# The first layer of a dense mixture by seven block products in place of eight

## The chip, the cores and the metric

One Trainium2 chip, one of its cores. The metric is the time of one execution on the device in microseconds (us); of several runs the median is given.

## What is computed

Three stages in a row: causal attention over 2 batches of 8 heads (576 tokens, 64 channels), a top-1 mixture of 8 experts, and a dense mixture of 4 experts, each over 1152 tokens of 512 channels. The change is in the third stage and in what the second hands to it.

```python
def _moe2_ref(x, domain_probs, w1, w2):       # x [1152, 512], w1 [4, 512, 1024], w2 [4, 1024, 512]
    p = domain_probs / (domain_probs.sum(-1, keepdims=True) + 1e-09)
    out = np.zeros((N, D), dtype=np.float32)
    for e in range(E):
        h = np.maximum(x @ w1[e], 0.0)
        out += p[:, e:e + 1] * (h @ w2[e])
    return out.astype(np.float32)
```

## The kernel before

The kernel is written with a scheduling layer: the Python text gives the work and the tiles, the layer sets the order of the instructions on each engine, the places in memory and the semaphores. On the chip each engine then works through its own list in that order. A pool with `bufs=n` holds n tiles of a tag; an instruction that takes a tile waits until the tile's last holder has been read.

**Float32 by halves.** In the dense stage, and for one expert of the top-1 stage, a float32 operand is split into a rounded part (`hi`, `xh`, `hh`; type float32r, made by ScalarE, ACT) and the rest (`lo`, `xl`, `hl`; made by VectorE, DVE). A product is then three float32r matmuls: hi by hi, hi by low, low by hi. The other seven experts of the top-1 stage use float32 matmuls, which the trace shows as two records each.

**The top-1 stage** (lines 700 to 830). Tokens are sorted by expert; slot `sl` of 8 has a fixed capacity (`CAPS`). `layer1` (L733 on) multiplies 8 tiles of F into PSUM tiles `pg` (3 buffers), read by ACT and DVE in turn; `layer2` (L765 on) makes 4 tiles `py` (3 buffers), and `put_y` (L760) writes each into `xh` and `xl`, the transposed and sorted input of the dense stage: ACT first, then DVE. Expert weights come by DMA on SyncE's queue (SP), in tiles `w` of 128 x 1024 (512 KB) from the pool `wp`, 17 buffers. Behind the last slot stands a branch (`tc.If(most > 0)`, L832) for tokens over capacity, which is not taken here.

**The dense stage** (L861 to L891). For each of 4 experts `e`, and for each third `g` of the tokens (384): the first layer makes 8 tiles of F, each from 4 tiles of D by 3 products, 12 matmuls of 384 columns into `pg`; ACT takes `hh`, DVE takes `hl` from it. The second layer then makes 3 tiles of 128 tokens, 24 matmuls of 512 columns each into `py`; DVE scales by the token's probability and adds into `acc` (the tile `X`). The weights of the next expert are split while the present one is worked on (`load_w`, `split_w`, L683 to L689). After the last expert each tile of tokens is scattered to its place in the output by GpSimd (POOL).

```python
for f in range(FC):
    pg = ps.tile([P, 512], F32, tag="g1", name="pg", bufs=3)
    ...
    for cc in range(KC):
        for wt, xt in ((whi, xh), (whi, xl), (wlo, xh)):
            nc.tensor.matmul(out=pg[:, :GN], lhsT=wt[:, cc, fs], rhs=xt[:, cc, cs], start=n == 0, stop=n == 3 * KC - 1)
```

Of the kernel before, what the change touches and what calls it, by code (L numbers as in the profile page):

```python
# [9 lines left out]
F32 = mybir.dt.float32  # L10
# [22 lines left out]
G = 3  # L33
GN = N // G
# [347 lines left out]
def tile_attention_moe_moe(  # L382
# [5 lines left out]
    wp = ctx.enter_context(tc.tile_pool(name="wp", bufs=17))  # L388
# [3 lines left out]
    X = con.tile([P, NT, DM], F32, name="X")  # L392
# [196 lines left out]
    mp = ctx.enter_context(tc.tile_pool(name="mp", bufs=1))  # L589
    hp_ = ctx.enter_context(tc.tile_pool(name="hp", bufs=9))  # L590
    ps = ctx.enter_context(tc.tile_pool(name="ps", bufs=2, space=PSUM))
# [32 lines left out]
    xh = mp.tile([P, KC, XW], F32R, name="xh")  # L624
    xl = mp.tile([P, KC, XW], F32R, name="xl")
# [107 lines left out]
    def layer1(pa, xs, cap, load=None):  # L733
        xs, xsl = xs
        split = xsl is not None
        hb = mp.tile([P, FC, GN], F32R if split else F32, tag="hh", name="hb")
        hbl = mp.tile([P, FC, GN], F32R, tag="hl", name="hbl") if split else None
# [55 lines left out]
    def rest(j):  # L793

        if j != 1:
            return
        for i in range(4):
            t = wp.tile([P, 2, DM], F32, tag="w", name="w")
# [13 lines left out]
    xs = turn_first(xw)  # L812
    for sl in range(E1):
# [12 lines left out]
        if not last:  # L826
            pa, pb = na, nb_

    ha, hb2 = load_w(u1[0], u2[0], True)


    with tc.If(most > 0):  # L832
        with tc.For_i(0, E1, 1) as sl:
# [4 lines left out]
            with tc.For_i(0, ov_r, P) as i:  # L838
# [8 lines left out]
                for dc in range(KC):  # L847
# [5 lines left out]
                    put_y(dc, py[:, :P], oo, P)  # L853


    acc = X
    for e in range(E2):
        if e:
            ha, hb2 = load_w(u1[e], u2[e], True)
        for g in range(G):  # L860
            cs = slice(g * GN, (g + 1) * GN)  # L861
            hh = mp.tile([P, FC, GN], F32R, tag="hh", name="hh")
            hl = mp.tile([P, FC, GN], F32R, tag="hl", name="hl")
            for f in range(FC):
                pg = ps.tile([P, 512], F32, tag="g1", name="pg", bufs=3)
                fs = slice((f % 2) * P, (f % 2) * P + P)
                whi, wlo = ha[f // 2]
                n = 0
                for cc in range(KC):
                    for wt, xt in ((whi, xh), (whi, xl), (wlo, xh)):  # L870
                        nc.tensor.matmul(out=pg[:, :GN], lhsT=wt[:, cc, fs], rhs=xt[:, cc, cs], start=n == 0, stop=n == 3 * KC - 1)  # L871
                        n += 1
                nc.scalar.activation(out=hh[:, f, :], in_=pg[:, :GN], func=AF.Relu)  # L873
                nc.vector.scalar_tensor_tensor(out=hl[:, f, :], in0=pg[:, :GN], scalar=0.0, in1=hh[:, f, :].bitcast(F32), op0=ALU.max, op1=ALU.subtract)  # L874
            for t in range(GN // P):
                tt = g * (GN // P) + t
# [12 lines left out]
                if e == E2 - 1:
                    scatter("out", out, aux.bitcast(I32)[:, tt, 4:5], acc[:, tt, :])  # L890
# [27 lines left out]
```

## Time and profile before

| | |
|---|---|
| median of 3 runs | 731.23 us (730.08 to 731.41) |
| the profiled execution, own time | 736.14 us |
| its span in the profile | 734.5 us |
| TensorE (PE) busy | 709.0 us, 97% |
| VectorE (DVE) busy | 269.4 us, 37% |
| ScalarE (ACT) busy | 210.5 us, 29% |
| clock granted to TensorE, mean | 0.98 |

The span is cut into three stretches: attention and routing until about 160 us, the top-1 stage until 327 us, the dense stage until the end. Matmuls are pipelined: a record of 338 ns overlaps the next one, so that PE's rate is read from the distance of starts, not from the mean duration. Times inside the profile are of one execution, which was 4.9 us above the median.

### The profile page before, as it was taken

To read this page: it belongs to the slowest core of one execution; us is meant where nothing else is said; L and a number is where in the kernel's file an instruction comes from. 1 tells how busy PE (TensorE), PEld (TensorE's weight loads), DVE (VectorE), ACT (ScalarE), POOL (GpSimd) and SP (SyncE) were. 2 spreads that over 40 slices of the span, in tenths; PEclk is the share of its full clock that TensorE was granted. 3 is DMA by queue.
4 is the path that set the end of the run, shared out by engine and by line. 5 is a ranking of instruction groups with operands and counts; after the bars stand their busy time and mean duration, and the time that the engine had idled before them with its cause. 6 is when DMAs were issued, how large, how long until landed. Compare 5 with 4: busy or idle time off the path is not lost.

```text
span 734.5 us, 11018 instructions
## 1 busy us (share of the span) xinstructions
PE 709.0 (97%) x4349; PEld 648.2 (88%) x4350; DVE 269.4 (37%) x724; ACT 210.5 (29%) x435; POOL 33.3 (5%) x72
## 2 busy tenths in 40 slices
PE   8899999969899999999999999999999999999996
PEld 5799999859799999989899898989898998989895
DVE  7586767642127111432122341214231133412121
ACT  5577767511125111331011230104120121302010
POOL 2000000033200000000000000000000000010101
PEclk9999999979899999999999999999999999999999
DMA  6656764049978976440001230003210011000001
GB/s 145 178 129 173 190 162 136 1 174 330 359 233 296 326 254 202 148 169 2 1 0 30 87 114 1 1 1 114 87 29 0 1 47 40 0 29 15 29 15 44
DMA packets 87006, 78.83 MB, mean 107 GB/s; under 512 B 42699, under 2 KB 67275, under 8 KB 86951
## 3 DMA queue, kind: packets, MB, share of 16 engines
q1 hardware_dynamic: 83063, 72.76, 32.5%
q0 software_dynamic: 1776, 4.79, 1.7%
q10 hardware_dynamic: 2112, 0.52, 0.4%
q8 instruction: 36, 0.59, 0.3%
q14 instruction: 19, 0.16, 0.1%
HBM read 69.08 MB, written 8.99 MB: 106 GB/s over the span
## 4 chain that ended last, share of the span: by engine, by line
PE 53%; issue 1%; POOL 0%; POOLq 0%; DVE 0%
PE pg L871 27%; PE py L883 26%; POOL out_dram L402 0%; POOLq L913 0%; DVE X L888 0%; POOLq L402 0%
## 5 line engine op out<-in xcount | busy, mean ns | idle before, releaser
L871 PE MATMUL pg<-xh,hi 128*128 128x384 f32 x384 | 129.3, 337 | 1.8 <-PEq L832 1.8
L871 PE MATMUL pg<-xl,hi 128*128 128x384 f32 x384 | 129.6, 338 | 0.0
L871 PE MATMUL pg<-xh,wl 128*128 128x384 f32 x384 | 128.8, 335 | 0.0
L873 ACT ACTIVATE hh<-pg 128x384 fp32r<-128x384 f32 x96 | 47.2, 492 | 277.5 <-PE pg L871 277.5
L883 PE MATMUL py<-wl,hh 128*128 128x512 f32 x288 | 113.9, 395 | 0.0
L883 PE MATMUL py<-hi,hh 128*128 128x512 f32 x288 | 113.1, 393 | 0.0
L883 PE MATMUL py<-hi,hl 128*128 128x512 f32 x288 | 112.9, 392 | 0.0
L874 DVE SCALAR_TENSOR_TENSOR hl<-pg,hh 128x384 fp32r<-128x384 f32 x96 | 53.5, 558 | 122.0 <-ACT hh L873 120.2
L871 PEld LDWEIGHTS pg<-xh,hi 128*128 128x128 f32 x384 | 71.9, 187 | 2.5 <-ACTq L832 2.0
L871 PEld LDWEIGHTS pg<-xl,hi 128*128 128x128 f32 x384 | 72.3, 188 | 0.5
L871 PEld LDWEIGHTS pg<-xh,wl 128*128 128x128 f32 x384 | 72.1, 188 | 0.1
L750 PE MATMUL pg<-xs,w 128*128 128x128 f32 (+6 forms) x448 | 65.2, 308 | 3.1 <-issue 3.0
L750 PEld LDWEIGHTS pg<-xs,w 128*128 128x128 f32 x448 | 63.3, 202 | 4.4 <-issue 4.0
L883 PEld LDWEIGHTS py<-hi,hh 128*128 128x128 f32 x288 | 54.1, 188 | 12.5
L883 PEld LDWEIGHTS py<-hi,hl 128*128 128x128 f32 x288 | 54.0, 188 | 12.5
L883 PEld LDWEIGHTS py<-wl,hh 128*128 128x128 f32 x288 | 54.0, 188 | 11.6
L888 DVE SCALAR_TENSOR_TENSOR X<-py,aux,X 128x512 f32<-128x512 f32 x27 | 20.3, 751 | 117.5 <-PE py L883 117.5
L775 PE MATMUL py<-hb,w 128*128 128x128 f32 (+6 forms) x448 | 61.3, 295 | 0.0
L775 PEld LDWEIGHTS py<-hb,w 128*128 128x128 f32 x448 | 59.4, 190 | 0.2
L688 DVE TENSOR_TENSOR wl<-w,hi 128x1024 fp32r<-128x1024 f32 x40 | 48.9, 1224 | 24.3 <-ACT hi L686 23.3
L686 ACT ACTIVATE hi<-w 128x1024 fp32r<-128x1024 f32 x40 | 42.1, 1054 | 40.0 <-PE py L883 34.1
L283 PE MATMUL av<-vt,ptT 128*128 128x65 f32 x320 | 46.6, 276 | 0.2 <-ACT ptT L271 0.2
(207 smaller groups left out, 803.3 us busy)
## 6 DMA issues: line engine op xcount, KB each, us to landing
w<-in_moe_w_dram SPq DMA_DIRECT2D x96, 512.0 KB
region<-zrow SPq DMA_DIRECT2D x8, 512.0 KB
bc<-ncum_d SPq DMA_DIRECT2D x7, 576.0 KB
ks<-in_k_dram SPq DMA_DIRECT2D x28, 128.0 KB
br<-ncum_d SPq DMA_DIRECT2D x16, 144.0 KB
qs<-in_q_dram SPq DMA_DIRECT2D x16, 128.0 KB
vt<-in_v_dram SPq DMA_DIRECT2D x16, 128.0 KB
xw<-region SPq DMA_DIRECT2D x8, 256.0 KB
```

What stands on the lines that cost most here:

```text
L283: nc.tensor.matmul(out=av[b][:, 65 * c : 65 * c + 65], lhsT=st[("pt", j)], rhs=d["vt"][:, j, b, :], start=j == 0, stop=j == c)
L686: nc.scalar.activation(out=hi, in_=t, func=AF.Copy)
L688: nc.vector.tensor_tensor(out=lo, in0=t, in1=hi.bitcast(F32), op=ALU.subtract)
L750: nc.tensor.matmul(out=pg[:, :cap], lhsT=wt[:, cc, fs], rhs=xt[:, cc, :cap], start=i == 0, stop=i == n - 1)
L775: nc.tensor.matmul(out=py[:, :cap], lhsT=wt[:, f % 2, dcs], rhs=ht[:, f, :cap], start=f == 0 and i == 0, stop=f == FC - 1 and i == len(pai ...
L871: nc.tensor.matmul(out=pg[:, :GN], lhsT=wt[:, cc, fs], rhs=xt[:, cc, cs], start=n == 0, stop=n == 3 * KC - 1)
L873: nc.scalar.activation(out=hh[:, f, :], in_=pg[:, :GN], func=AF.Relu)
L874: nc.vector.scalar_tensor_tensor(out=hl[:, f, :], in0=pg[:, :GN], scalar=0.0, in1=hh[:, f, :].bitcast(F32), op0=ALU.max, op1=ALU.subtract)
L883: nc.tensor.matmul(out=py, lhsT=ht[:, f, ts_], rhs=wt[:, f % 2, :], start=n == 0, stop=n == 3 * FC - 1)
L888: nc.vector.scalar_tensor_tensor(out=acc[:, tt, :], in0=py, scalar=aux[:, tt, e : e + 1], in1=acc[:, tt, :], op0=ALU.mult, op1=ALU.add)
```

## The change

The sorted input of the dense stage stays in float32 (`xf`, in the place of `X`), and the splitting moves behind it. The dense stage works on 8 units: an expert and a half of F (512). In a unit the first layer runs over two chunks `c` of 576 tokens, and in each over two groups `p` of 256 rows of F. Such a piece, 256 of F by 512 of D by 576 tokens, is a product of 2 x 2 by 2 x 2 blocks (blocks of 128 by 256 by 288), and is made by Strassen's method in Winograd's form: 7 block products of 6 matmuls with 288 columns, in place of 8. It needs four sums of weight blocks for each `p` (`wsum`, L870 to L873, by DVE) and four sums of input blocks for each chunk (`tsum`, L648), which are split into hi and low like the operands themselves. `build(0)` stands behind the seventh slot of the top-1 stage, `build(1)` behind the branch. The products are added up partly in PSUM and partly in SBUF (`t`): of each piece ACT copies four (L943) and DVE adds three (L946); then one relu by ACT (L950) and one subtraction by DVE (L951), 1152 elements wide, give `hh` and `hl`. The second layer follows for all 9 tiles of tokens, 12 matmuls of 512 columns each, with one addition into `acc` per tile and unit, 72 in place of 36. PSUM has two buffers each of `qa`, `qb`, `qd` and of `py`; before there were three each of `pg` and `py`. Weight buffers: `wp` 11 and, in the top-1 stage alone, `wq` 6 for fixed places in the sequence; `hi` tiles 6, before 9. `put_y` writes a tile once, by ACT or DVE in turn. POOL clears a part of `xf` (L841) before the first slot's results.

```diff
-    wp = ctx.enter_context(tc.tile_pool(name="wp", bufs=17))
+    wp = ctx.enter_context(tc.tile_pool(name="wp", bufs=11))
...
-            t = wp.tile([P, KC, 256] if i < 4 else [P, 2, DM], F32, tag="w", name="w")
+            t = (wq if i in (1, 4, 6) else wp).tile([P, KC, 256] if i < 4 else [P, 2, DM], F32, tag="w", name="w")
...
-        nc.scalar.activation(out=xh[:, dc, ds(off, cap)], in_=y, func=AF.Copy)
-        nc.vector.tensor_tensor(out=xl[:, dc, ds(off, cap)], in0=y, in1=xh[:, dc, ds(off, cap)].bitcast(F32), op=ALU.subtract)
+        if dc % 2:
+            nc.vector.tensor_copy(out=xf[:, dc, ds(off, cap)], in_=y)
+        else:
+            nc.scalar.activation(out=xf[:, dc, ds(off, cap)], in_=y, func=AF.Copy)
...
+    def build(c, tmp):
...
+        base = (blk(0, 0), blk(1, 0), blk(1, 1))
+        pairs = ((0, blk(0, 1), blk(0, 0)), (2, blk(1, 1), blk(0, 1)), (1, blk(1, 1), t[:, 0]), (3, blk(1, 0), t[:, 1]))
+        for i in range(4):
+            if i < 3:
+                nc.scalar.activation(out=bh[:, i], in_=base[i], func=AF.Copy)
+                nc.vector.tensor_tensor(out=bl[:, i], in0=base[i], in1=bh[:, i].bitcast(F32), op=ALU.subtract)
+            j, a, b = pairs[i]
+            nc.vector.tensor_tensor(out=t[:, j], in0=a, in1=b, op=ALU.subtract)
+            nc.scalar.activation(out=th[:, j], in_=t[:, j], func=AF.Copy)
+            nc.vector.tensor_tensor(out=tl[:, j], in0=t[:, j], in1=th[:, j].bitcast(F32), op=ALU.subtract)
...
+    def halves(e, h):
...
+            nc.vector.tensor_tensor(out=g[:, 0], in0=a(1, 0), in1=a(1, 1), op=ALU.add)
...
+            first.append((split_w(t), split_w(g.rearrange("p i k f -> p (i k) f"))))
...
+    def product(name, out, w, x, start):
...
+        for k in range(2):
...
+            for a, b in ((wh, xh), (wh, xl), (wl, xh)):
+                nc.tensor.matmul(out=out[:, :HT], lhsT=a, rhs=b, start=start and n == 0, stop=n == 5, skip_group_check=True)
...
+        for name in ("P1", "P2", "P6", "P7", "P5", "P4", "P3"):
+            for p in range(2):
+                qa, qb, qd, t = qs[p]
+                q = {"P2": qb, "P7": qd, "P4": qd}.get(name, qa)
+                product(name, q, w[p], ops[c], name in ("P1", "P2", "P7"))
...
+                    nc.scalar.activation(out=t[:, i], in_=y, func=AF.Copy)
...
+                    nc.vector.tensor_tensor(out=t[:, i], in0=y, in1=t[:, i], op=ALU.add)
```

Three places where the order of the instructions is another one follow.

**The end of a unit's first layer, on DVE.** Before, in the dense stage, DVE takes `hl` of each tile of F, three additions after each third of the tokens, and one low part of a weight tile now and then:

```order
L874 SCALAR_TENSOR_TENSOR hl<-pg,hh 128x384 x8
L888 SCALAR_TENSOR_TENSOR X<-py,aux,X 128x512 x3
L874 SCALAR_TENSOR_TENSOR hl<-pg,hh 128x384
L688 TENSOR_TENSOR wl<-w,hi 128x1024
L874 SCALAR_TENSOR_TENSOR hl<-pg,hh 128x384 x3
```

Now, from the last two additions of products (`qd`) to the second layer's tiles (`py`):

```order
L946 TENSOR_TENSOR t<-qd,t 128x288 x2
L713 TENSOR_TENSOR wl<-w,hi 128x1024
L713 TENSOR_TENSOR wl<-wsum,hi 128x1024
L951 SCALAR_TENSOR_TENSOR hl<-t,hh 128x2x576 x2
L870 TENSOR_TENSOR wsum<-w 128x256
L872 TENSOR_TENSOR wsum<-w 128x256
L871 TENSOR_TENSOR wsum<-wsum,w 128x256
L713 TENSOR_TENSOR wl<-w,hi 128x1024
L873 TENSOR_TENSOR wsum<-w,wsum 128x256
L978 SCALAR_TENSOR_TENSOR acc<-py,aux,acc 128x512 x2
L713 TENSOR_TENSOR wl<-wsum,hi 128x1024
L978 SCALAR_TENSOR_TENSOR acc<-py,aux,acc 128x512 x6
```

The low parts and sums of the next unit's weights now stand ahead of the first addition into `acc`, which frees a `py` buffer. On PE, at the same place, behind the second tile of tokens (`py_4650`) and six matmuls of the next unit's P1 for p = 0 (`qa_4764`):

```order
L927 MATMUL qa_4768<-xbh0_3619,hi_4616 128x288
L927 MATMUL qa_4768<-xbl0_3620,hi_4616 128x288
L927 MATMUL qa_4768<-xbh0_3619,wl_4618 128x288
L927 MATMUL qa_4768<-xbh0_3619,hi_4616 128x288
L927 MATMUL qa_4768<-xbl0_3620,hi_4616 128x288
L927 MATMUL qa_4768<-xbh0_3619,wl_4618 128x288
L927 MATMUL qb_4765<-xbh0_3619,hi_4601 128x288
L973 MATMUL py_4664<-hi_4235,hh_4372 128x512
```

So 13 matmuls of the next unit stand between the second and the third tile of tokens; `py_4664`, the third, takes the first one's buffer.

**Between the two chunks of a unit, on ACT.** `t_4377` and `t_4381` are the sums of chunk 0 for p = 0 and 1, `t_4487` and `t_4491` those of chunk 1; the first two rows copy P3 of chunk 0's two groups, each with its relu:

```order
L943 ACTIVATE t_4377<-qa_4374 128x288
L950 ACTIVATE hh_4372<-t_4377 128x2x576
L943 ACTIVATE t_4381<-qa_4378 128x288
L950 ACTIVATE hh_4372<-t_4381 128x2x576
L943 ACTIVATE t_4487<-qa_4484 128x288
L943 ACTIVATE t_4491<-qa_4488 128x288
L943 ACTIVATE t_4487<-qa_4484 128x288
```

The copy that frees `qa` of p = 1 stands behind the relu of p = 0, and the first copy of chunk 1 behind the relu of p = 1. Before, ACT had one instruction for each tile of F there (`hh<-pg`).

**The last slot of the top-1 stage, on ACT.** Before, from the last result of the seventh slot (172 columns) on:

```order
L762 ACTIVATE xh<-py 128x172
L757 ACTIVATE hb<-pg 128x188 x2
L686 ACTIVATE hi<-w 128x1024
L757 ACTIVATE hb<-pg 128x188
L686 ACTIVATE hi<-w 128x1024
L757 ACTIVATE hb<-pg 128x188
```

Now:

```order
L790 ACTIVATE xf<-py 128x172
L711 ACTIVATE hi<-wsum 128x1024
L645 ACTIVATE xbh_3619<-xf 128x576 x2
L782 ACTIVATE hb<-pg 128x188
L649 ACTIVATE xth_3621<-tsum 128x576
L711 ACTIVATE hi<-w 128x1024
L649 ACTIVATE xth_3621<-tsum 128x576
L782 ACTIVATE hb<-pg 128x188
L649 ACTIVATE xth_3621<-tsum 128x576
L782 ACTIVATE hb<-pg 128x188 x2
```

Copies of `build(0)` now stand between the reads of the last slot's `pg` tiles.

## Rows read from the trace of the kernel before

**Rows 1.** The page: busy time of each engine; PE's granted clock in 40 slices.

```profile
PE 709.0 (97%) x4349; PEld 648.2 (88%) x4350; DVE 269.4 (37%) x724; ACT 210.5 (29%) x435; POOL 33.3 (5%) x72
...
PEclk9999999979899999999999999999999999999999
```

**Rows 2.** The chain that ended last, merged: start, length in us, what.

```profile
344.31 16.66 PE py L883 x72
360.97 16.77 PE pg L871 x96
...
695.23 16.77 PE pg L871 x96
```

**Rows 3.** Waits: who waited for whom, us in total, times, longest.

```profile
ACT hh L873 <- PE pg L871: 277.5, 93, 18.3
```

**Rows 4.** Line 750, 200 to 345 us: min/median/max ns, first and last start.

```profile
L750 PE MATMUL pg<-xs,hi x32: 274/278/370, 223.5 to 234.2; 128*128 128x248 f32 x32
...
L750 PE MATMUL pg<-xs,wl x32: 273/278/280, 223.8 to 234.4; 128*128 128x248 f32 x32
```

**Rows 5.** Groups of instructions on ACT by shape: count, busy us, mean ns.

```profile
L686 ACT ACTIVATE hi<-w 128x1024 fp32r<-128x1024 f32 x40 | 42.1, 1054 | 40.0 <-PE py L883 34.1 <-PE pg L871 4.3 <-DMA w<-in_moe_w_dram 1.6
...
L164 ACT ACTIVATE ql<-qs 128x576 fp32r<-128x576 f32 x7 | 4.7, 678 | 0.2 <-DMA qs<-in_q_dram 0.2
...
L704 ACT ACTIVATE xs<-tp 128x288 f32<-128x288 f32 x1 | 0.4, 411 | 0.5 <-PE tp L701 0.5
```

**Rows 6.** The same on DVE.

```profile
L688 DVE TENSOR_TENSOR wl<-w,hi 128x1024 fp32r<-128x1024 f32 x40 | 48.9, 1224 | 24.3 <-ACT hi L686 23.3 <-DVEq L832 0.9
L888 DVE SCALAR_TENSOR_TENSOR X<-py,aux,X 128x512 f32<-128x512 f32 x27 | 20.3, 751 | 117.5 <-PE py L883 117.5
...
L165 DVE SCALAR_TENSOR_TENSOR ql<-qs,ql 128x576 fp32r<-128x576 f32 x7 | 5.3, 752 | 0.1
...
L763 DVE TENSOR_TENSOR xl<-py,xh 128x248 f32 x4 | 1.7, 417 | 10.0 <-ACT xh L762 10.0
...
L165 DVE SCALAR_TENSOR_TENSOR ql<-qs,ql 128x256 fp32r<-128x256 f32 x2 | 0.7, 406 | 0.0
```

**Rows 7.** Timeline (start, us): from PE to ACT and DVE in the dense stage.

```profile
429.60 0.33 PE L871 MATMUL pg<-xh,wl 128*128 128x384 f32 x1
...
429.97 0.49 ACT L873 ACTIVATE hh<-pg 128x384 fp32r<-128x384 f32 x1 [3.83 <-PE pg L871]
...
430.50 0.56 DVE L874 SCALAR_TENSOR_TENSOR hl<-pg,hh 128x384 fp32r<-128x384 f32 x1 [0.76 <-ACT hh L873]
```

**Rows 8.** Timeline, 155 to 167.5 us: from ACT to PE.

```profile
166.03 0.38 ACT L726 ACTIVATE xs<-tp 128x256 f32<-128x256 f32 x1 [11.23 <-PE tp L724]
...
166.47 1.44 PE L750 MATMUL pg<-xs,w 128*128 128x128 f32 x5 [0.15 <-ACT xs L726]
```

**Rows 9.** Timeline: instructions that follow on DVE, and on ACT, without a wait.

```profile
220.56 1.23 DVE L688 TENSOR_TENSOR wl<-w,hi 128x1024 fp32r<-128x1024 f32 x1 [0.16 <-ACT hi L686]
221.70 0.72 DVE L763 TENSOR_TENSOR xl<-py,xh 128x144 f32 x2
...
320.52 0.33 ACT L762 ACTIVATE xh<-py 128x188 f32 x1 [2.22 <-PE py L775]
320.74 1.05 ACT L686 ACTIVATE hi<-w 128x1024 fp32r<-128x1024 f32 x1
```

**Rows 10.** Timeline of PE, 320 to 329 us: the last slot's end, the branch.

```profile
319.68 5.89 PE L775 MATMUL py<-hb,w 128*128 128x188 f32 x36
327.32 0.41 PE L871 MATMUL pg<-xh,hi 128*128 128x384 f32 x1 [1.75 <-PEq L832]
```

**Rows 11.** Windows: us, PE, PEld, DVE, ACT, POOL busy; clock, DMA share, GB/s.

```profile
240.00:260.00 20.00, 20.00 (x161) 19.29 (x160) 3.37 (x10) 3.04 (x9) 0.00 (x0) 1.00 1.03 330
```

**Rows 12.** POOL: a group of its instructions; its timeline in the first slot.

```profile
L417 POOL MEMSET zrow<- 128x512 f32 x1 | 0.5, 538 | 0.0
...
178.12 0.96 POOL L402 DMA_INDIRECT aux_d<-ax,cpi  x1 [10.02 <-DVE cpi L672]
```

More of the change, by code (lines that the diff above doesn't have):

```diff
@@ L827, in tile_attention_moe_moe @@
             pa, pb = na, nb_
-    ha, hb2 = load_w(u1[0], u2[0], True)
+        if sl == E1 - 2:
+            build(0, (mp, "hl"))
+    def halves(e, h):
+        first, second = [], []
+        for p in range(2):
+            t = wp.tile([P, KC, 256], F32, tag="w", name="w")
+            load_a(t, u1[e], 2 * h + p)
+            g = wp.tile([P, 4, 2, P], F32, tag="w", name="wsum")
+            a = lambda i, j: t[:, 2 * j : 2 * j + 2, i * P : (i + 1) * P]
+            nc.vector.tensor_tensor(out=g[:, 0], in0=a(1, 0), in1=a(1, 1), op=ALU.add)
+            nc.vector.tensor_tensor(out=g[:, 1], in0=g[:, 0], in1=a(0, 0), op=ALU.subtract)
+            nc.vector.tensor_tensor(out=g[:, 2], in0=a(0, 0), in1=a(1, 0), op=ALU.subtract)
+            nc.vector.tensor_tensor(out=g[:, 3], in0=a(0, 1), in1=g[:, 1], op=ALU.subtract)
+            first.append((split_w(t), split_w(g.rearrange("p i k f -> p (i k) f"))))
+        for p in range(2):
+            t = wp.tile([P, 2, DM], F32, tag="w", name="w")
+            load_b(t, u2[e], 2 * h + p)
+            second.append(split_w(t))
+        return first, second
+    wa, wb = halves(0, 0)
     with tc.If(most > 0):
@@ new lines, in tile_attention_moe_moe @@
+        build(0, (mp, "hl"))
+    top1.close()
+    mp2 = ctx.enter_context(tc.tile_pool(name="mp2", bufs=1))
+    ps2 = ctx.enter_context(tc.tile_pool(name="ps2", bufs=2, space=PSUM))
+    PROD = {
+        "P1": ((0, 0), (0, 0)), "P2": ((1, 0), (0, 1)), "P3": ((None, 3), (0, 2)), "P4": ((1, 1), (1, 3)),
+        "P5": ((None, 0), (1, 0)), "P6": ((None, 1), (1, 1)), "P7": ((None, 2), (1, 2)),
+    }
+    def product(name, out, w, x, start):
+        (j, i), (kind, m) = PROD[name]
+        (base, sums_) = w
+        n = 0
+        for k in range(2):
+            wh, wl = (t[:, 2 * i + k, :] if j is None else t[:, 2 * j + k, i * P : (i + 1) * P] for t in (sums_ if j is None else base))
+            xh, xl = (t[:, m, k, :] for t in x[2 * kind : 2 * kind + 2])
+            for a, b in ((wh, xh), (wh, xl), (wl, xh)):
+                nc.tensor.matmul(out=out[:, :HT], lhsT=a, rhs=b, start=start and n == 0, stop=n == 5, skip_group_check=True)
+                n += 1
@@ new lines, in first_layer @@
+    def first_layer(c, w, hh, hl):
+        qs = []
+        for p in range(2):
+            qa, qb, qd = (ps2.tile([P, 512], F32, tag=n, name=n) for n in ("qa", "qb", "qd"))
+            qs.append((qa, qb, qd, mp2.tile([P, 4, HT], F32, tag="t", name="t", bufs=2)))
+        for name in ("P1", "P2", "P6", "P7", "P5", "P4", "P3"):
+            for p in range(2):
+                qa, qb, qd, t = qs[p]
+                q = {"P2": qb, "P7": qd, "P4": qd}.get(name, qa)
+                product(name, q, w[p], ops[c], name in ("P1", "P2", "P7"))
+                y = q[:, :HT]
+                if name in ("P1", "P6", "P7", "P3"):
+                    i = {"P1": 0, "P6": 2, "P7": 3, "P3": 1}[name]
+                    nc.scalar.activation(out=t[:, i], in_=y, func=AF.Copy)
+                else:
+                    i = {"P2": 0, "P5": 3, "P4": 2}[name]
+                    nc.vector.tensor_tensor(out=t[:, i], in0=y, in1=t[:, i], op=ALU.add)
+        for p in range(2):
+            t = qs[p][3].rearrange("p (i b) t -> p i (b t)", i=2)
+            r = (slice(None), slice(2 * p, 2 * p + 2), slice(2 * HT * c, 2 * HT * c + 2 * HT))
+            nc.scalar.activation(out=hh[r], in_=t, func=AF.Relu)
+            nc.vector.scalar_tensor_tensor(out=hl[r], in0=t, scalar=0.0, in1=hh[r].bitcast(F32), op0=ALU.max, op1=ALU.subtract)
@@ new lines, in tile_attention_moe_moe @@
+    acc = None
+    units = [(e, h) for e in range(E2) for h in range(2)]
+    for u, (e, h) in enumerate(units):
+        hh = mp2.tile([P, 4, N], F32R, tag="hh", name="hh")
+        if u == 0:
+            build(1, (mp2, "hl"))
+        hl = mp2.tile([P, 4, N], F32R, tag="hl", name="hl")
+        for c in range(2):
+            first_layer(c, wa, hh, hl)
+        if u + 1 < len(units):
+            na, nb_ = halves(*units[u + 1])
+        if acc is None:
+            acc = big.tile([P, NT, DM], F32, tag="X", name="acc")
+        for tt in range(NT):
+            ts_ = slice(tt * P, (tt + 1) * P)
+            py = ps2.tile([P, 512], F32, tag="g2", name="py")
+            n = 0
+            for f in range(4):
+                whi, wlo = wb[f // 2]
+                for ht, wt in ((hh, whi), (hh, wlo), (hl, whi)):
+                    nc.tensor.matmul(out=py, lhsT=ht[:, f, ts_], rhs=wt[:, f % 2, :], start=n == 0, stop=n == 11)
+                    n += 1
+            if u == 0:
+                nc.vector.tensor_scalar(out=acc[:, tt, :], in0=py, scalar1=aux[:, tt, e : e + 1], scalar2=None, op0=ALU.mult)
+            else:
+                nc.vector.scalar_tensor_tensor(out=acc[:, tt, :], in0=py, scalar=aux[:, tt, e : e + 1], in1=acc[:, tt, :], op0=ALU.mult, op1=ALU.add)
+            if u == len(units) - 1:
+                scatter("out", out, aux.bitcast(I32)[:, tt, 4:5], acc[:, tt, :])
+        if u + 1 < len(units):
+            wa, wb = na, nb_
```

67 lines of the change are left out of this document (22 added, 45 removed).

## The prediction

> **What bounds the kernel now.** Read the page first: PE is busy for 97% of the span, DVE for 37% and ACT for 29%, and the clock line shows nine tenths of full speed or more in every slice behind the top-1 stage [rows 1] (1.00 where a window gives it, that is 2.4 GHz [rows 11]). Then the chain: in the dense stage it is nothing but PE, pieces of the first layer and pieces of the second in turn, twelve of each [rows 2]. The waits say the same from the other side: ACT stood 277.5 us idle until a tile of the first layer was done [rows 3], and DVE 117.5 us until a tile of the second was [rows 6]. So only what PE does, or what makes PE wait, counts. Its rate is the distance of starts. A first-layer piece has 96 matmuls of 384 columns in 16.77 us, 174.7 ns each; a second-layer piece has 72 of 512 columns in 16.66 us, 231.4 ns each [rows 2]. A matmul of 248 columns in the same form of float32r stands in the top-1 stage: 96 starts from 223.5 to 234.4 us, 114.7 ns apart [rows 4]. These three lie on one line: 60.0 ns for 136 columns, 0.441 ns a column, between the first and the second; 56.7 ns for 128, 0.443, between the second and the third. At 288 columns that gives 114.7 + 40 x 0.441 = 132.4 ns.
>
> **The change, part by part.** Sums are made against the profiled execution's own 736.14 us; the median of the runs shown, 731.23, lies 4.9 us lower, and I take the same difference from it.
>
> *First layer, on PE.* Removed: 12 pieces of 16.77 us, 201.2 us for 1152 matmuls. Added: 8 units x 2 chunks x 2 groups x 7 products x 6 = 1344 matmuls of 132.4 ns, 177.9 us. Gain 23.3 us. The starts in rows 4 are given to 0.1 us, which is 1 ns in the distance: +-1.3 us.
>
> *Second layer, on PE.* 864 matmuls of 512 columns as before. The 72 additions into `acc` of 0.75 us in place of 36 [rows 6] are DVE's, 27 us more on an engine that is idle for most of the stage; but the place of the first of them matters.
>
> For the walks below I need durations. ACT: 0.41 us for a copy of 288 columns, 1.05 for 1024, and by the line from 576 to 1024 1.16 for the 1152 of the relu [rows 5]. DVE: 1.22 for a low part, 0.41 for a sum of 256, by the line from 256 to 576 1.38 for the 1152 of `hl`, 0.75 for an addition into `acc` [rows 6]. ACT began 0.2 us after the end of its matmul's interval (429.60 + 0.175), DVE 0.04 after ACT [rows 7], PE 0.06 after ACT [rows 8]. An instruction that has nothing to wait for starts about 0.09 us before the one ahead of it ends [rows 9].
>
> *Third tile of the second layer (the DVE list).* Time 0 is the end of the last product on PE. P4 of p = 0 ended 2.4 us earlier (three products of 0.79), and only then are the hi buffers free for the next unit's weights. ACT splits two of them until -0.2, and then owes copy, relu, copy, relu: done at 2.8. DVE's second `hl` ends at 4.2; three sums, a low part, a sum and the addition follow, 3.6 us less six overlaps: 7.3. PE meanwhile has two tiles, 24 x 231.4 ns = 5.55, and 13 matmuls of the next unit, 1.72: it wants the first `py` buffer at 7.27. With the hand-over PE stands for 0.1 us, at 7 unit ends about 1 us. Ends: nothing, where the queue runs a little faster; 0.85 us each, 6 us, where nothing overlaps. Behind the late addition stand the second tile's, and one low part; they have a tile's time of 2.8 us each.
>
> *Between the chunks (the ACT list).* P3 of p = 0 ends at -0.79. Copy, relu, copy: the buffer of p = 1 is free at 1.35. PE has P1 of p = 0 and half of P2, 1.19 us, and waits 0.2. The copy of the new P1 of p = 1 needs its `t`, which the second `hl` is read from until 4.0: done at 4.5, where PE wanted it at about 4.2; again 0.3. That is 0.5 at each of 8 places, 4 us. Ends: 0, since each wait is as small as a hand-over, and 8 us, where nothing overlaps.
>
> *The rest of the additions in a chunk* have cover: a product takes 0.79 us, and each `qa` or `qd` is written again at the earliest two products later, 1.6 us, against 0.2 + 0.41 us for the copy, or 0.46 for DVE's addition (417 ns at 248 columns [rows 6]).
>
> *Last slot of the top-1 stage (the ACT list).* A tile of F takes 8 records of 0.16 us there (36 in 5.89 [rows 10]), 1.28 us. The fifth tile waits for the buffer of the third, read by ACT: PE is there at 4 x 1.28, plus four records of the second layer that stand between, 5.8 us after the slot's start. ACT starts on `build(0)` once DVE has copied the previous slot's last tile, at about 1.1; two copies and two parts of 576 (0.68 each), a weight tile (1.05), two relus (0.33 [rows 9]) are 4.4 less 0.6 of overlaps, with some 2 us of waits for DVE's subtractions, which stand behind low parts of 1.22: about 7.0. PE loses 1.2 us. Ends: 0, where DVE is ahead, and 3, where a weight tile lands late in between.
>
> *The branch.* Before, PE stood 1.75 us there [rows 10]; ACT and DVE have about as much to finish now. `build(1)` needs 11 DVE instructions of 0.75, about 7.5 us with overlaps, while PE has a whole chunk, 84 x 132.4 ns = 11.1 us, before it needs the first of it; the additions behind it in the queue come late. I take 0.3 us, ends 0 and 1.
>
> *Costed at nothing.* POOL's clearing of 4 x 576 columns: 538 ns for 512 [rows 12], so about 2.4 us for 2304; POOL idles for 10.0 us ahead of 178.12 [rows 12], and the first result is written at about 177. If that cover went, the first slot would lose up to 2.4 us. The weight loads: between 240 and 260 us the DMA engines are full (share 1.03) while PE is busy all 20 us [rows 11], so they run ahead of it; with 11 and 6 buffers for 17 a load starts at most about a slot's layer later than before. The dense stage loads the same bytes. The end is the same, one tile's addition and scatter.
>
> Sum: -23.3 + 1.0 + 4.0 + 1.2 + 0.3 = **-16.8 us**: 719.3 for the profiled execution, **714.4 us** from the median.
>
> **A rule against it.** The rows give a matmul almost no price of its own: 231.4 - 512 x 0.443 = 4.6 ns. The Trainium skill (TensorE: Matmul & The Clock Gate, Back-to-back issue gap) says that in a stream of weight loads and matmuls the sustained spacing is about 81 ns at 128 columns and 131 at 512. By an estimate from these figures 288 columns would take 102 ns and 384 114, the new layer 136.8 us and the old one 131.7, a loss of 5 us. The trace does not agree: 231.4 ns at 512 columns [rows 2].
>
> **The rivals.**
> *Everything hides.* DVE and ACT come a few tenths earlier than walked; the gain is the 23.3 us: 707.9. For it: each wait is 0.1 to 0.3 us, and both engines are idle for most of the span [rows 1]. Against: 15 places that the lists make tight. 0.15.
> *The queues hold PE.* ACT and DVE overlap less than in rows 9, and all waits come to their upper ends: -23.3 + 6 + 8 + 3 + 1 = -5.3, 725.9; with the worse rate 727.2. For it: the lists are in order, and an instruction that waits stops those behind it. 0.22, of which 0.02 has no measurable gain.
> *Slower: the third tile becomes the place that sets the pace.* Where the chain of sums and low parts on DVE ends not at 7.3 but past 10.9 us, 7 stops of over 3.6 us outweigh the rest; at 4.5 us each it is 731.2 - 23.3 + 5.5 + 31.5 = 745. It would take a weight tile that lands late: the sums read the second `w` of the next unit. Against: its load is issued when the buffer of a weight tile split in the middle of chunk 0 is free, some 16 us ahead. 0.06.
> *Slower: a matmul has a price of its own.* If the distance at 288 columns were over 149.7 ns, 201.2 us / 1344, the new layer would be the longer one; a fixed part of 100 ns, with 0.195 ns a column, gives 156 ns, 209.8 us, and 731.2 + 8.6 + 6.5 = 746. Rows 2 and 4 speak against it: 114.7 ns at 248 columns, and the slope between any two of the three. 0.02. The Trainium skill's rule above is of this kind.
>
> **How the numbers follow.** My forecast has 0.55, the rivals 0.15, 0.22, 0.06 and 0.02. A change of 0.2% (1.5 us) is about what a measurement of this kernel can tell from none. Faster: 0.55 + 0.15 + 0.20 = 0.90; the same: 0.02; slower: 0.06 + 0.02 = 0.08. The range reaches from all of the gain with the better end of the rate, 731.2 - 24.6 = 706.6, to the upper ends with the worse one, -4.0, 727.2; I take 706.5 to 727. The slow rivals and a part of the held queues lie outside.
>
> **What would show it.** The distance of the 288-column matmuls between 131 and 134 ns; the first layer's share of the chain down by 23 us and the second's unchanged; PE's idle time in the dense stage at two places of a unit, the P1 and P6 matmuls of p = 1 in chunk 1 (waiting for ACT) and the third `py` tile (waiting for DVE), together under 1 us a unit; a gap of about 1 us in the last slot. I am wrong in the rate if the distance is over 140 ns, and in the queues if PE waits over 2 us a unit.

## The result, and the profile after

Measured: 713.64 us, median of 4 runs (711.88 to 715.48), against 730.65 of the kernel before on the same chip (729.63 to 731.41). The ratio is 0.9768, 95% interval 0.9739 to 0.9797: 17.0 us faster. The forecast was 714.4, range 706.5 to 727.0.

The page of the changed kernel, beside [rows 1]:

```profile
PE 688.8 (97%) x4541; PEld 623.9 (88%) x4542; DVE 374.5 (53%) x878; ACT 267.7 (38%) x513; POOL 35.4 (5%) x73
...
PEclk9899999978999999999999999999999999999999
...
PE py L973 27%; PE qa L927 15%; PE qd L927 7%; PE qb L927 4%; POOL out_dram L403 0%; POOLq L1005 0%; DVE acc L978 0%; POOLq L403 0%
```

DVE went from 37% to 53% of a shorter span and ACT from 29% to 38%, and the chain is still PE: 26 points of first layer (`qa`, `qd`, `qb`) and 27 of second (`py`). One unit of it, from the chain (start, length in us, what), beside [rows 2]:

```profile
380.50 2.38 PE qa L927 x18
382.88 0.40 PE qb L927 x3
...
383.29 1.06 PE qa L927 x6
384.35 1.19 PE qb L927 x9
...
392.08 1.59 PE qa L927 x12
393.67 5.57 PE py L973 x24
399.24 1.59 PE qa L927 x12
400.83 0.13 PE qb L927
400.96 9.14 PE py L973 x39
```

Twelve matmuls of 288 columns in 1.587 us are 132.2 ns each. The second layer's first piece starts at 393.67 here and at 680.62 six units later, so the unit's period is 286.95 / 6 = 47.83 us.

**Which trace of before to subtract.** The profiled execution of before lay 4.9 us over its median. Its dense stage ran from 327.32 us on; in the kernel before, profiled again, it starts at 321.98 and is just as long (below). Against that second trace (span 729.1) the changed kernel's span is 17.6 us shorter. Its dense stage, from 322.88 to the end of the second layer's last piece, takes 382.8 us where before took 401.4, 18.5 us less; it starts 0.9 us later. Three things make up the 0.9. The top-1 stage begins 2.0 us later (168.83 against 166.87). Its first slot and the second slot's first layer take 24.4 us against 26.1, nearly all of it in the first slot's first layer: 7.41 us at a mean granted clock of 1.00 against 9.04 us at 0.81, which is not the change's doing, since the version with the copies first (below) has 9.03 again. And 0.7 us is lost from there to the branch.

What is left of waits in the dense stage, on PE's weight loads (PEld; who waited for whom, us in total, times, longest):

```profile
PEld qa L927 <- ACT t L943: 3.2, 16, 0.2
```

Sixteen waits, two a unit; the timeline of one unit (start, length in us, engine, line, operation) shows where:

```profile
382.99 0.29 PE L927 MATMUL qb<-xbh,wl 128*128 128x288 f32 x1
383.29 0.40 PE L927 MATMUL qa<-xbh,hi 128*128 128x288 f32 x1
383.53 0.29 PE L927 MATMUL qa<-xbl,hi 128*128 128x288 f32 x1
...
386.17 0.29 PE L927 MATMUL qd<-xth,hi 128*128 128x288 f32 x1
386.39 0.40 PE L927 MATMUL qa<-xth,hi 128*128 128x288 f32 x1
386.63 0.29 PE L927 MATMUL qa<-xtl,hi 128*128 128x288 f32 x1
```

and ACT and DVE in the same stretch:

```profile
381.77 1.17 ACT L950 ACTIVATE hh<-t 128x1152 fp32r<-128x1152 f32 x1
...
382.85 0.39 ACT L943 ACTIVATE t<-qa 128x288 f32<-128x288 f32 x1
382.98 2.86 DVE L951 SCALAR_TENSOR_TENSOR hl<-t,hh 128x1152 fp32r<-128x1152 f32 x2 [0.94 <-ACT hh L950]
383.27 1.17 ACT L950 ACTIVATE hh<-t 128x1152 fp32r<-128x1152 f32 x1
...
385.93 0.85 ACT L943 ACTIVATE t<-qa 128x288 f32<-128x288 f32 x2 [1.09 <-DVE hl L951]
```

These are the two places that the prediction walked: P1 of p = 1 waits for the copy that stands behind the relu (382.85), and P6 of p = 1 waits for the first of the two copies that wait for DVE's second `hl` (385.93). From start to start the first costs 0.54 us for two matmuls in place of 0.26, the second 0.46: 0.28 and 0.20 us. The wait itself is only part of it; the matmul behind a waiting weight load is followed 0.11 us later than usual (0.24 in place of 0.13).

### The profile page after: what moved, and what is told of

Its sections match the earlier page's. It is cut to its first block, busy times and chain, and to the rows that moved or that the text cites. A ratio compares the mean times of both kernels' runs of the same rounds, so it can differ in the third digit from the quotient of the medians.

```text
span 711.5 us, 11689 instructions
## 1 busy us (share of the span) xinstructions
PE 688.8 (97%) x4541; PEld 623.9 (88%) x4542; DVE 374.5 (53%) x878; ACT 267.7 (38%) x513; POOL 35.4 (5%) x73
## 4 chain that ended last, share of the span: by engine, by line
PE 53%; issue 1%; POOL 0%; POOLq 0%; DVE 0%
PE py L973 27%; PE qa L927 15%; PE qd L927 7%; PE qb L927 4%; POOL out_dram L403 0%; POOLq L1005 0%; DVE acc L978 0%; POOLq L403 0%
## 5 line engine op out<-in xcount | busy, mean ns | idle before, releaser
L978 DVE SCALAR_TENSOR_TENSOR acc<-py,aux,acc 128x512 f32<-128x512 f32 x63 | 46.6, 748 | 84.6 <-PE py L973 84.6
L943 ACT ACTIVATE t<-qa 128x288 f32<-128x288 f32 x96 | 37.9, 404 | 65.4 <-PE qa L927 56.5
L775 PE MATMUL pg<-xs,w 128*128 128x128 f32 (+6 forms) x448 | 60.2, 295 | 0.4 <-ACT hb L782 0.2
L951 DVE SCALAR_TENSOR_TENSOR hl<-t,hh 128x1152 fp32r<-128x1152 f32 x32 | 43.4, 1357 | 13.7 <-ACT hh L950 11.6
L258 ACT ACTIVATE p<-p,mn 128x512 f32<-128x512 f32 (+4 forms) x72 | 40.6, 582 | 10.5 <-DVE mn L246 9.9
L283 PEld LDWEIGHTS av<-vt,ptT 128*128 128x128 f32 x320 | 43.5, 201 | 0.7 <-ACT ptT L271 0.5
L271 ACT ACTIVATE ptT<-pt 128x512 f32<-128x512 f32 (+3 forms) x80 | 34.3, 435 | 19.5 <-PE pt L269 19.2
L927 PE MATMUL qa<-xbh,hi 128*128 128x288 f32 x128 | 38.5, 301 | 1.5 <-PEq L884 1.4
L927 PE MATMUL qa<-xth,hi 128*128 128x288 f32 x128 | 38.5, 301 | 0.0
L246 DVE CUSTOM_DVE_ANT_0 p<-sc,p 128x512 f32<-128x512 f32 (+4 forms) x72 | 34.6, 484 | 7.0 <-PE sc L209 4.7
```

Source lines behind the costliest of these rows:

```text
L246: self.last[1] = nc.vector.tensor_tensor_reduce(out=t[:, lo : lo + w], in0=st["sc"][:, 0:w], in1=t[:, lo : lo + w], scale=1.0, scalar=init ...
L258: self.last[0] = nc.scalar.activation(out=t[:, 0:w], in_=t[:, 0:w], func=AF.Exp, scale=-1.0, bias=st["mn"][:, 0:1])
L283: nc.tensor.matmul(out=av[b][:, 65 * c : 65 * c + 65], lhsT=st[("pt", j)], rhs=d["vt"][:, j, b, :], start=j == 0, stop=j == c)
L775: nc.tensor.matmul(out=pg[:, :cap], lhsT=wt[:, cc, fs], rhs=xt[:, cc, :cap], start=i == 0, stop=i == n - 1)
L927: nc.tensor.matmul(out=out[:, :HT], lhsT=a, rhs=b, start=start and n == 0, stop=n == 5, skip_group_check=True)
L943: nc.scalar.activation(out=t[:, i], in_=y, func=AF.Copy)
```

## The experiments

**The kernel before, once more** (no edit).

> The kernel before, profiled once more. My reading of the two traces: of the 6.8 us by which the top-1 stretch of the changed kernel was shorter (160.85 us from the first matmul of the stretch to the first of the dense stage, against 154.05), about 7 belong to the one profiled execution of before, whose first two slots took 31.6 us against 24.4 at a granted clock of 0.83. Then this profile has a top-1 stretch of 153 to 155 us and a dense stage of 401.3 +-1 us, and the slots 0 and 1 take 24 to 26 us. Rival: the change itself shortened the top-1 stage (float32 hand-over, one pass of put_y instead of two); then the stretch is again 159 us or more here, and 5 to 7 us of the 17 us are not the block products' at all.

Measured: 730.81 us (one run). Chain:

```profile
321.98 17.01 PE pg L871 x96
338.99 16.66 PE py L883 x72
355.64 16.77 PE pg L871 x96
```

The top-1 stretch took 155.1 us (166.87 to 321.98) in place of 160.85. Its beginning, which the expectation calls the first two slots and which reaches to the end of the second slot's first layer, took 26.1. Both are 0.1 us over the expected ranges, and far from the rival's 159. The dense stage is unchanged at 401.4. In the first profile of before PE stands in the second slot's first layer, without anything that the trace names as cause:

```profile
184.34 0.73 PE L750 MATMUL pg<-xs,w 128*128 128x136 f32 x4 [0.27 <-issue]
187.28 2.71 PE L750 MATMUL pg<-xs,w 128*128 128x136 f32 x10 [2.21 <-issue]
```

In the same place the granted clock was 0.50 for some us (a window of 3 us; from and to, length, busy us of PE, PEld, DVE, ACT, POOL, granted clock, DMA share, GB/s):

```profile
187.00:190.00 3.00, 2.71 (x10) 2.31 (x10) 0.22 (x1) 0.00 (x0) 1.89 (x2) 0.50 1.07 381
```

So these 5.3 us belong to that execution, not to the change (a version of the changed kernel has the same stop, below), and the dense stage has to answer for the whole of the 17 us.

**Eight block products.** The seven are replaced:

```diff
-        for name in ("P1", "P2", "P6", "P7", "P5", "P4", "P3"):
...
+        for i in range(2):
+            for k in range(2):
+                for p in range(2):
...
+                    for j in range(2):
+                        product(q, (j, i), w[p], X[j, k], ops[c], j)
...
+                    nc.scalar.activation(out=hh[r], in_=q[:, :HT], func=AF.Relu)
```

> The changed kernel with eight block products: the same units, chunks, 288 columns and second layer, but each output block is made of its two products in PSUM, 12 matmuls, and ACT and DVE take hh and hl straight from there; no weight sums, no tile t. The input block sums are still made and one is replaced by a plain copy. Theory (the gain is the eighth product, the rest of the restructuring is worth little): 1536 matmuls of 132.25 ns are 203.1 us, 25.4 more than the 1344; the waits between the chunks, 3.7 us, should go with the shorter ACT list: 713.6 + 25.4 - 3.7 = 735, range 734 to 740, so 4 to 9 us slower than the kernel before. Rival (units, hand-over in float32 and the larger second-layer stretches bring a good part): under 728.

Measured: 734.55 us (732.12 to 735.31), ratio to before 1.0061 (1.0045 to 1.0076). In its chain the first layer of a unit is one piece without a wait:

```profile
371.46 25.38 PE q L924 x192
396.85 25.06 PE py L961 x108
```

25.38 us against 22.68 in the changed kernel (the period of 47.83 less 25.15 of second layer): the eighth product is worth 2.7 us a unit, 21.6 in all, more than the whole gain, and the restructuring without it is 4.6 us slower than the kernel before. Of these, 1.8 are matmuls (8 x 25.38 us against 201.2) and 0.6 the second layer (8 x 25.06 against 199.9); the other 2.2 do not show in its profiled execution, which was the fastest of four, and stay open.

**Copies first, and three buffers of `t`.**

```diff
-            qs.append((qa, qb, qd, mp2.tile([P, 4, HT], F32, tag="t", name="t", bufs=2)))
+            qs.append((qa, qb, qd, mp2.tile([P, 4, HT], F32, tag="t", name="t", bufs=3)))
...
-                    nc.scalar.activation(out=t[:, i], in_=y, func=AF.Copy)
+                    cp = nc.scalar.activation(out=t[:, i], in_=y, func=AF.Copy)
...
-            nc.scalar.activation(out=hh[r], in_=t, func=AF.Relu)
+            with tc.issue_after(cp.ins):
+                nc.scalar.activation(out=hh[r], in_=t, func=AF.Relu)
```

> Two edits between the chunks: ACT copies the last product of both groups before it begins the two relus, and the tile t has three buffers instead of two. Theory (the 0.46 us a unit that the first layer loses between its chunks are ACT's order and the buffers of t): the P1 matmul of p = 1 no longer waits, the P6 matmul of p = 0 at most 0.1 us; the unit's period falls from 47.83 to 47.4 to 47.5 us, the time by 2.5 to 3.5 us, 710 to 711.5. Rival (the loss is PE's own hand-over at each change of PSUM bank or weights, not ACT): the period stays within 0.1 us of 47.83, and the time within 0.7 us of 713.6. Second rival (the relus come later, and the second layer or DVE's hl now wait): period over 47.9, time over 714.3.

Measured: 708.37 us (706.44 to 709.92), ratio 0.9695 (0.9678 to 0.9711). The border between the chunks, and the second layer's start:

```profile
380.46 3.17 PE qa L927 x24
383.63 1.59 PE qb L927 x12
...
393.15 5.57 PE py L974 x24
```

The 24 matmuls across the chunks' border take 3.17 us, no longer with a wait; the period is 47.37 us. The wait is gone as the theory has it, but the time fell by 5.3 us, 1.6 below the expected range. Run once more beside the changed kernel:

> The changed kernel once more, beside the version with both edits (copies first, three buffers of t) on the same chip, since the two stood in different comparisons before. Theory (the version gains what the traces show, 7 periods of 0.455 us and 0.46 in the first unit, 3.65 us): this kernel is 3.2 to 4.2 us slower than the other, its ratio to the kernel before 0.974 to 0.979. Rival (the 5.3 us between the two medians, 713.64 and 708.37, are real, with 1.6 us outside the dense stage): 4.8 us or more.

> The version with both edits, on the same chip as the changed kernel: 3.2 to 4.2 us faster than that; its unit's period 47.37 us again, against 47.83. If the difference is 4.8 us or more, something outside the dense stage gained too.

Measured: 712.36 us (710.26 to 717.9; ratio 0.9766, 0.9731 to 0.9801) and 708.34 us (708.2 to 711.32; ratio 0.9712, 0.9686 to 0.9737): 4.0 us between them, inside the expected 3.2 to 4.2. The runs of the two spread over 7.6 and 3.1 us, so the medians alone do not tell 4.0 from the rival's 4.8. The traces do: the periods are 47.83 and 47.35 us, 3.4 us over seven of them, and the first unit is 0.45 shorter, 3.8 in all. With both edits the kernel is 2.9% under the kernel before, the fastest version tried.

**The two edits apart.** The order alone:

> Of the two edits of the run with the copies first and three buffers of t, only the order: ACT's copies of the last products ahead of the relus, t with two buffers. Theory (t's buffers are the second of two causes): the P1 matmul of p = 1 no longer waits, but the next chunk's first copy waits for DVE's read of the old t, until about 3.15 us after the last product, and PE wants that qa buffer after 3.17 less what the copy takes: P6 of p = 0 waits about 0.3 us a unit. The unit's period is 47.6 to 47.75 us (47.83 in the changed kernel, 47.37 with both edits), the time 711 to 713. Rival (the order alone is the cause): period 47.4, time 708.4 to 709.5.

Measured: 714.66 us (712.67 to 715.95; ratio 0.9783, 0.9755 to 0.9811), period 47.75 us. The period is as expected, the time 1.7 us over its range. The wait of P1 is gone and the one behind it took its place; the chain runs through ACT and DVE now:

```profile
384.41 1.17 ACT hh L951
...
385.60 1.37 DVE hl L952
...
387.05 0.42 ACT t L943
...
387.52 1.06 PE qa L927 x6
```

In the profiled run (714.63 us) most of the time's miss lies in the first unit, which took 24.4 us from its first matmul to the second layer, where the changed kernel took 23.0: behind the branch PE's granted clock was half (windows as above).

```profile
324.00:326.00 2.00, 2.00 (x13) 2.00 (x12) 2.00 (x4) 2.00 (x4) 0.00 (x0) 0.65 0.30 98
326.00:328.00 2.00, 2.00 (x10) 2.00 (x10) 2.00 (x4) 0.75 (x3) 0.00 (x0) 0.50 0.00 0
328.00:332.00 4.00, 4.00 (x32) 4.00 (x32) 2.48 (x5) 2.07 (x6) 0.00 (x0) 1.00 0.00 0
```

The buffers alone:

> The other half of the run with both edits: three buffers of t, the order of ACT's copies and relus left to the scheduling layer, which now puts the next chunk's first copy between the two relus. Theory (two causes, one wait each: the P1 matmul of p = 1 waits for ACT's copy behind the relu of p = 0, the P6 matmul of p = 1 for DVE's read of the old t): the second wait goes, the first stays at 0.2 us: the unit's period falls from 47.83 to 47.55 to 47.65 us, the time to 711 to 712.5, between the changed kernel and the 708.4 of both edits. Rival (the buffers alone are the cause, the order follows): period 47.4, time 708 to 709.5.

Measured: 716.86 us, but on a chip on which the kernel before took 737.08 in the median of seven runs; the ratio is 0.9716 (0.9692 to 0.974). Its profile has the stop of the second slot too (`issue`, 3.3 us), so its time says little, and the period decides: 47.63 us, as expected for one wait of two; the waits on `t` from 350 us on are 7 where the changed kernel has 14. So 47.83, 47.75 (order), 47.63 (buffers), 47.37 (both): neither edit alone brings half of it, because the order alone moves the second wait to P6 of p = 0, and the buffers alone leave the first.

**A later addition, in the second layer.**

```diff
+    scr = mp2.tile([P, 2, 512], F32, name="scr")
...
+            if tt == 0 and 0 < u:
+                nc.vector.tensor_scalar(out=scr, in0=py.unsqueeze(1).to_broadcast([P, 2, 512]), scalar1=1.0, scalar2=None, op0=ALU.mult)
```

> The changed kernel with one more DVE instruction in each unit from the second on: the first py tile is read twice over into a scratch tile of 128 x 1024, about 1.3 us, ahead of its addition into acc; by the order DVE also does one low part of a weight tile, 1.22 us, ahead of that addition. So the first py buffer is free some 2.3 us later (1.3 + 1.22 less two overlaps of 0.09). Theory (the third tile of the second layer is just in time now, with no slack): at 7 unit ends PE waits 2.2 to 2.5 us, 15 to 18 us in all: 729 to 731. Rival (there is slack that the trace does not show, PE runs on with other matmuls): within 3 us of 713.6. This is also the mechanism of the slow rival of the prediction, tried at a known size.

Measured: 713.22 us (712.65 to 713.8), no change: the expectation failed. The addition was late as planned, 402.32 in place of 399.99 us:

```profile
399.97 1.22 DVE L977 TENSOR_SCALAR scr<-py 128x1024 f32<-128x1024 f32 x1
401.18 1.23 DVE L713 TENSOR_TENSOR wl<-wsum,hi 128x1024 fp32r<-128x1024 f32 x1
402.32 1.41 DVE L981 SCALAR_TENSOR_TENSOR acc<-py,aux,acc 128x512 f32<-128x512 f32 x2
```

but the scheduling layer had put 30 matmuls of the next unit ahead of the third tile, not 13, and PE came to it at 403.1:

```profile
393.67 5.58 PE py L974 x24
399.25 1.58 PE qa L927 x12
400.83 1.59 PE qb L927 x12
402.42 0.79 PE qa L927 x6
403.21 0.86 PE py L974 x3
```

The order is made anew for each kernel. So the run does not show slack; it shows that a delay which the layer knows of is filled with other work. To test the walk, the filling has to be forbidden.

**No cover.** The matmuls of the next unit that stand ahead of the third tile are its cover: PE has them to do while DVE is late. Here each matmul of the first layer is ordered behind the last one of the second layer of the unit before:

```diff
-                product(name, q, w[p], ops[c], name in ("P1", "P2", "P7"))
+                with tc.issue_after(behind.ins) if behind is not None else ExitStack():
+                    product(name, q, w[p], ops[c], name in ("P1", "P2", "P7"))
...
+                    end = nc.tensor.matmul(out=py, lhsT=ht[:, f, ts_], rhs=wt[:, f % 2, :], start=n == 0, stop=n == 11)
```

> The changed kernel with one order imposed: no matmul of the next unit's first layer may stand ahead of the last matmul of this unit's second layer. The lists of DVE and ACT stay as they were, so the first addition into acc ends as before, 7.07 us after the second layer's first matmul, and the first py buffer is wanted after two tiles, 5.57 us. Theory (the 13 matmuls between the second and the third tile are the cover of DVE's late addition, which runs on the clock that I walked): PE waits 7.13 - 5.57 = 1.56 us at each of 7 unit ends, 10.9 us: 713.4 + 10.9 = 724.3, range 722 to 727. Rival (DVE's list gives way, and the additions were not what the order was made for): within 2 us of 713.4.

Measured: 724.67 us (723.28 to 727.95), ratio 0.9938 (0.9915 to 0.9961). PE's waits:

```profile
PE py L974 <- DVE acc L979: 9.1, 6, 1.5
PE py L974 <- DVE acc L977: 1.5, 1, 1.5
```

1.5 us at each of 7 places, as walked (1.56), and the chain leaves PE there: two splits and two copies by ACT, the relu, `hl`, three sums, a low part, a sum, the addition. That is the list of the prediction, and its cover is worth about 11 us.

**No weight sums.** The products read other slices of the plain weights where they should read the sums:

```diff
-            nc.vector.tensor_tensor(out=g[:, 0], in0=a(1, 0), in1=a(1, 1), op=ALU.add)
...
-            first.append((split_w(t), split_w(g.rearrange("p i k f -> p (i k) f"))))
+            first.append((split_w(t), None))
...
-            wh, wl = (t[:, 2 * i + k, :] if j is None else t[:, 2 * j + k, i * P : (i + 1) * P] for t in (sums_ if j is None else base))
+            wh, wl = (t[:, i, k * P : (k + 1) * P] if j is None else t[:, 2 * j + k, i * P : (i + 1) * P] for t in base)
```

> The changed kernel without the four weight sums of each group and without their split; the products that should use the sums use other slices of the plain weights, so that their number and shape stay. What Strassen's method costs on DVE and ACT beside PE is taken away: 4 x 0.42 + 1.22 us of DVE and 1.05 us of ACT for each of 16 groups, 46 us of DVE in all. Theory (it is hidden but for the third tile, which was just in time, and some tenths in the last slot): 712.5, range 711 to 713.6, the unit's period at 47.7 to 47.83. Rival (the sums hold PE at places that the waits do not name, among them memory traffic): under 710.

Measured: 711.50 us (709.56 to 712.77; ratio 0.9734, 0.9709 to 0.9759), period 47.77 us. Instructions of 46 us on DVE and 17 on ACT are taken away (busy time on the page, without overlaps: DVE 374.5 to 336.2, ACT 267.7 to 252.3), and the unit is 0.06 us shorter: the sums are hidden. The order gave way here as well: no matmul of the next unit stands inside the second layer, which is one piece of 25.05 us. In the profiled run (712.77 us) the first unit lost 1.5 us to the granted clock (24.5 us against 23.0; last section), so that the period says more than the time.

**Half columns.**

```diff
-                nc.tensor.matmul(out=out[:, :HT], lhsT=a, rhs=b, start=start and n == 0, stop=n == 5, skip_group_check=True)
+                for z in (slice(0, HT // 2), slice(HT // 2, HT)):
+                    nc.tensor.matmul(out=out[:, z], lhsT=a, rhs=b[:, z], start=start and n == 0, stop=n == 5, skip_group_check=True)
```

> The changed kernel with each block-product matmul cut into two of 144 columns: 2688 instead of 1344, the same columns in all; each cut loads its weights again. Theory (the distance of starts is 0.443 ns a column and 4.6 ns a matmul, as read from 248, 384 and 512 columns): 68.4 ns each, 183.9 us for the first layer instead of 177.8: 719.5, range 717 to 723. Rival (a matmul has a price of its own that wider ones hide): a fixed price of 100 ns and more gives 128 ns each, 344 us, 879; in between lies a floor, the weight load, whose records take 188 ns each but overlap: at 100 ns a matmul 269 us, 804. By the Trainium skill (TensorE: Matmul & The Clock Gate, Back-to-back issue gap), as an estimate from its figures for 128 and 512 columns, it would be 83 ns each, 223 us.

Each half starts an accumulation of its own in the PSUM tile, and the result is not the reference's; only the number and shape of the matmuls count here.

Measured: 839.43 and 872.29 us in two runs. The theory's line fell, and the rival of a floor fits, with another number. At full clock 24 matmuls of 144 columns take 2.68 us:

```profile
430.63 2.68 PE qa L928 x24
433.31 2.68 PE qd L928 x24
```

That is 111.7 ns each, not 68.4. The estimate of 83 ns by the Trainium skill (TensorE: Matmul & The Clock Gate, Back-to-back issue gap) does not hold here either. 2688 x 111.7 = 300.2 us, 122.5 more than 1344 x 132.2; with 5.2 us of waits for the second layer's first buffer that is 841, and 839.43 was the shorter run. In the other, which is the profiled one, the clock was half in the first unit (mean granted clock 0.945 against 0.986 in the shorter run):

```profile
320.00:324.00 4.00, 1.99 (x16) 1.73 (x14) 1.56 (x3) 1.22 (x3) 0.00 (x0) 1.00 0.44 136
...
328.00:392.00 64.00, 64.00 (x302) 64.00 (x301) 14.03 (x23) 12.05 (x21) 0.00 (x0) 0.50 0.01 2
...
396.00:400.00 4.00, 4.00 (x18) 3.25 (x17) 2.49 (x3) 0.07 (x1) 0.00 (x0) 0.95 0.25 80
```

The floor is below the line at 248 columns (114.7 ns, line 114.4; [rows 4]); by an estimate from the line the two meet near 242: (111.7 - 4.6) / 0.443. 144 is the only width of float32r that was tried below that. But the attention stage of the kernel before has narrower matmuls of plain float32, each record with a weight load of its own, eight of 65 columns and eight of 8 columns in a row:

```profile
70.93 1.06 PE L283 MATMUL av<-vt,ptT 128*128 128x65 f32 x8
60.87 1.01 PE L496 MATMUL pl<-wg,xt 128*128 128x8 f32 x8
```

At a granted clock of 1.00 the median distance of starts is 112 ns in both lines. So a floor of this size could have been read from the trace before the change. The Trainium skill (TensorE: Matmul & The Clock Gate, LDWEIGHTS) gives a weight load as its columns divided by 1.2, in ns, which for 128 columns makes an estimate of 107 ns. The floor of 111.7 ns lies 4% above that. That the weight load is what sets it was not tried by itself.

## Why the prediction was right

- **First layer on PE, -23.3.** Measured 1344 x 132.2 = 177.7 us against 201.2: -23.5. The distance had been 132.4. Here the prediction stood on less than it knew: its line is right from 248 columns up, and 248 was 6 columns above the floor. With each matmul cut in two the layer grew by some 123 us, five times what the seven products save.
- **Between the chunks, +4.0.** A unit's first layer takes 22.68 us, its 168 matmuls 22.22: 0.46 us, 3.7 in all, at the two places named. The sizes were 0.28 and 0.20 where the walk had 0.2 and 0.3, and the two edits together take them away, so that the mechanism is shown and not only the sum.
- **Third tile, +1.0.** The addition was walked to end at 7.3 us after the last product; the first of two ended at 400.74, 7.1, and PE came at 7.1. The next distance is 0.33 in place of 0.23, 0.1 us at 7 places, 0.7. So it is just in time, as walked, and the run without cover shows what the cover hides: 1.5 us each, 10.6 in all.
- **Second layer, nothing.** 8 x 25.06 us without interleaved matmuls (the run of eight products) is 200.5 against 199.9 before: +0.6, the one cost that the prediction had not.
- **Last slot, +1.2.** The term that was mis-sized. PE stood 0.2 us:

```profile
306.58 5.36 PE L775 MATMUL pg<-xs,w 128*128 128x188 f32 x32 [0.21 <-ACT hb L782]
```

  From start to start (306.05, 306.58, 306.84, where 0.16 us is the distance without a wait) it cost 0.5. ACT began 0.9 us after the slot's start and let the third tile go at 6.05, not 7.0; it waited 0.9 us for DVE, not 2, and 0.2 for a weight tile.
- **The branch, +0.3.** PE stood 1.39 us, and 1.96 in the second profile of the changed kernel, where the two traces of before have 1.75 and 1.55: no loss shows.
- **At nothing.** POOL's clearing took 2.02 us (estimate 2.4), from 174.73 on, behind 4.25 us of idle time; PE's waits for weights in the top-1 stage are 0.6 us in both kernels. Its loss of 0.7 us from the second slot to the branch includes the 0.5 of the last slot; the rest was not followed up.

Sum by the traces: -23.5 + 3.7 + 0.7 + 0.6 in the dense stage, -18.5, and 0.9 later at its start: -17.6, where -16.8 was forecast and the medians give -17.0. That the sums lie so close is in part luck. The dense stage's own terms were right: -18.3 forecast, -18.5 measured. But the 1.5 us forecast for the last slot and the branch were 0.5 and nothing, and the rest of the difference between the two spans is made of parts that the prediction did not have: a top-1 stage that began 2.0 us later, for which no cause was looked for, and 1.7 us that it got back, nearly all by the granted clock.

**The rivals.** That everything hides (707.9) fell in this kernel, but is about what the version with both edits reaches (708.4). That queues hold PE at their upper ends fell: 0.46 us a unit, not 1. The slow rival by the third tile asked for a chain past 10.9 us; a chain that the scheduling layer knows to be 2.3 us longer cost nothing, and without cover the present one costs 1.5 us a unit. The slow rival by a price per matmul was wrong at 288 columns, and right in kind for narrow ones: at 144 columns a matmul cost 111.7 ns, and float32 records of 65 and of 8 columns stand 112 ns apart.

## What to carry to other kernels

Trade columns against matmuls only down to the width at which the distance of starts stops falling, and measure that floor, in narrow matmuls that the kernel already has if there are any: here 288 columns lay above it and half of them far below. When a chain of small waits stands between two stretches of the bounding engine, look for both its causes, an order in a list and a buffer that is still read: here the one edit alone moved a wait, and the other left one. And a late instruction that the scheduler's own model knows of is filled with other work, so that a delay put into the program tests the scheduler first and the slack second.

## What was not expected of the hardware

The floor of 111.7 ns for a float32r matmul of 144 columns, against a line of 4.6 + 0.443 ns a column that holds at 248, 288, 384 and 512; float32 records of 65 and 8 columns show the same floor. A PE wait costs more than its length: behind a waiting weight load the next matmul came 0.11 us late, so that a wait of 0.17 us cost 0.28. And the granted clock behind PE's stop at the branch: it fell to 0.50 (1.2 GHz) after a stop of 1.85 us in the run with the order alone, 2.10 us in the one without weight sums and 2.01 us in the one with half columns; it did not after 1.38 to 1.75 us in the others, nor after 1.92 and 1.96 us (three buffers of `t`; the second profile of the changed kernel), so the length of the stop alone does not tell. With 288 columns it was back at 1.00 within some 4 us and the fall cost 1.4 and 1.5 us. With 144 columns it stayed at 0.50 to the end of the unit's first layer, some 70 us, and was at 0.95 behind the first matmuls of 512 columns. At 0.50 the 144-column matmuls stood 212 ns apart (302 in 64.00 us), 100 ns more than at full clock; over the 336 of a first layer that is 34 us, about the 33 us between the two runs.
